# Query order, band factor, store shape and the slot of the mixture in an attention and adapter kernel

## The chip, the cores and the metric

The kernel runs on one core of one Trainium2 chip. The metric is the device time in microseconds (us) of one execution, as the median over runs. A core has five engines with a queue of their own each: TensorE (PE, with its weight loads as PEld), VectorE (DVE), ScalarE (ACT), GpSimd (POOL) and SyncE (SP, which here only issues DMA transfers). An engine works through its queue in order. A wait at the head holds up all that is behind it.

## The reference

Eight batches of eight heads, 576 positions, head dimension 64. Attention with a bias that depends on the distance alone, then per token a mixture of two of eight rank-16 adapters.

```
scores = scale * q @ k^T + bias_table[bucket(|i - j|)]     # bucket is constant from distance 128 on
attn   = softmax(scores);  y = attn @ v
x      = y as (4608 tokens, 512)
logits = x @ w_gate;  keep the two largest of 8;  w = softmax over the two
out    = x + sum over the two of  w_e * (x @ A_e) @ B_e
```

## The kernel before

**Attention.** Heads go in pairs: four pairs to a batch, 32 in all, numbered i, with `hp = i % 4`. The first 512 positions are the main part, the last 64 the tail. The scores of a pair lie transposed, keys on the partitions, in five groups of 1024 columns: groups 0 to 3 are 128 keys each of both heads against 512 queries, group 4 holds the tail keys and the tail queries. PE makes a group (`qk`), ACT takes the exponential (`expo`), DVE multiplies what lies near the diagonal by a band factor exp(bias) (`band`), PE multiplies with V (`pv`), and DVE divides (`recip`, `norm`) into a tile `x` of the batch.

**Order of positions.** A load gives partition p the four positions 4p to 4p+3 (j = 0 to 3), and PE transposes each j by itself (`transposes`). K and Q were both put back into natural order there: column 32j+u of a block of 128 is the position 4u+j of that block. So a batch's output rows lie j by j, and four stores are needed for two blocks (`m_out`).

**The loop.** It runs over slots n = 5i + g, g from 0 to 4, one per group. In what follows (hp, g) names a slot of a batch. Each slot says which instructions are recorded, and each engine's queue is in the order of the recording: no scheduler changes it. Engines have no clock of slots: SP, PE and DVE run ahead until a wait stops them.

**The mixture** of batch b is spread over the slots of the following batches by a table of events (`mixture`): when the last pair of b is done, in slot (0, 4) of batch b+1, one DMA on SP transposes x into `xT` (`m_xdma`; the last batch does it with 16 PE transposes and two DVE copies instead, `m_x`). Then, before the change: `m_logits` in (2, 0), the gates in (2, 2) to (2, 4), `m_z` in (3, 0) and (3, 2), `m_zT` in (3, 4), and in batch b+2 `m_out` in (0, 0), (0, 2), (1, 0), (1, 2). For every second batch the tails of two batches are done together (`m_xtail`, and `m_outt` with its tile `ot`).

**Loads.** SP issues in each batch, for the batch after it: K and Q (1 MB each), V in 16 pieces of 64 KB, 8 of them in slot (0, 0), 4 in (1, 0) and 4 in (2, 0). The same queue holds the xT transposes and all stores. Eight semaphores are handed out in turn to the DMAs of SP and ACT, and a DMA waits until the one eight places ahead of it has landed. POOL casts K, Q and V to bf16 (`cast_kq`, `cast_v`): V of pair i+1 in the last slot of pair i, ahead of the gate's own last step, which is also on POOL.

**The start.** The band factor goes through DRAM: DVE builds a small table (`g_sb`), ACT takes its exponential (`ge`), stores it (`g_d`), SP loads it back shifted by partition (`Mr`), and DVE or POOL copy it in order (`bias_pair`) into `M`. Half of the first batch's V was loaded from ACT's queue.

Of the kernel before, what the change touches and what calls it, by code (L numbers as in the profile page):

```python
# [27 lines left out]
def kernel(  # L28
# [14 lines left out]
    nc = tc.nc  # L43
    B, H, S, D = q.shape
# [8 lines left out]
    S4 = 512  # L53
    MW = 384
# [3 lines left out]
    cp = ctx.enter_context(tc.tile_pool(name="const", bufs=1))  # L58
# [6 lines left out]
    op = ctx.enter_context(tc.tile_pool(name="outs", bufs=3))  # L65
# [3 lines left out]
    ident = cp.tile([128, 128], BF16, tag="ident")  # L69
# [16 lines left out]
    dve = Recorder(nc.vector)  # L86
# [41 lines left out]
    def load_tail(b, w, e):  # L128
        sr = (k, q, v)[w][b, :, S4:, :].rearrange("(c e) p d -> e p c d", e=2)
        s = slice(e * 64, (e + 1) * 64)  # L130
        o = (tls[b % 2][s, w, :, s] if w < 2 else
             vts[b % 2][s, :, e * D1:e * D1 + D])
        nc.gpsimd.dma_start(out=o, in_=sr[e])
# [3 lines left out]
    def cast_kq(i, w, eng=None):  # L137
        b, hp = divmod(i, HP)
        if w == 0:
            kqn[i] = knp.tile([128, 2, 4, 2, D], BF16, name="kqn", tag="kqn")  # L140
        o = kqn[i][:, w].rearrange("p j h d -> p h j d")
        s = kfs[b][w][:, 2 * hp:2 * hp + 2, :].rearrange("p h (j d) -> p h j d", j=4)
        if eng is nc.scalar:
            for h in range(2):
                nc.scalar.copy(o[:, h], s[:, h])
        else:
            return (eng or nc.gpsimd).tensor_copy(o, s)  # L147
# [8 lines left out]
    btT = cp.tile([H, NB], FP32, tag="btT")  # L156
    nc.sync.dma_start(out=btT, in_=bias_table.rearrange("b h -> h b"))
    load_kq(0, 0, 2)
    load_v(0, (0, 1), nc.scalar)
    for t in tls[:1] + vts[:1]:  # L160
        dve.memset(t, 0.0)
    dve.memset(vns[0][:, :, :, D:D1], 1.0)
    for w in range(2):
        for e in range(2):
            load_tail(0, w, e)
    load_kq(0, 2, 4)
    load_v(0, (2, 3))
    load_kq(0, 4, 6)
# [24 lines left out]
    for bv, lo, hi in runs[nsm:]:  # L193
        n = hi - lo
# [6 lines left out]
    g_d = nc.dram_tensor("g_d", (H, 512), BF16, kind="Internal")  # L201
    nc.scalar.dma_start(out=g_d.ap(), in_=ge)
    cast_kq(0, 0, dve)
    cast_kq(0, 1, nc.scalar)
    cast_kq(1, 0, dve)
    cast_kq(1, 1, dve)
    gt = g_d.ap()
# [1 line left out]
    Mr = cp.tile([128, H, MW], BF16, tag="Mr")  # L209
    MHr = cp.tile([128, HP, 192], BF16, tag="MHr")  # L210
    for h0, h1 in ((0, 2), (2, 4), (4, H)):
        for j in range(4):
            nc.sync.dma_start(
                out=Mr[j * 32:(j + 1) * 32, h0:h1, :],
                in_=bass.AP(tensor=gt.tensor, offset=gt.offset + h0 * 512 + j,
                            ap=[[4, 32], [512, h1 - h0], [1, MW]]))
        if h0 == 0:
            for e in range(2):
                nc.sync.dma_start(
                    out=MHr[e * 64:(e + 1) * 64],  # L220
# [4 lines left out]

    M = cp.tile([128, H, 3, 128], BF16, tag="M")
    M4 = cp.tile([128, HP, 256], BF16, tag="M4")
    MHT = cp.tile([128, HP, 2, 64], BF16, tag="MHT")  # L230

    def at(t, off, *dims):
        return bass.AP(tensor=t.tensor, offset=t.offset + off,
                       ap=[t.ap[0]] + [list(d) for d in dims])

    def bias_pair(hp, eng):
        for blk in (1, 2, 0):
            eng.tensor_copy(
                M[:, 2 * hp:2 * hp + 2, blk, :].rearrange("p h (j u) -> p h j u", j=4),
                at(Mr, 2 * hp * MW + MW - 1 - 128 * blk, (MW, 2), (-1, 4), (-4, 32)))  # L240
        eng.tensor_copy(
            M4[:, hp, 0:128].rearrange("p (j u) -> p j u", j=4),
            at(MHr, hp * 192 + 191, (-1, 4), (-4, 32)))
        eng.tensor_copy(
            M4[:, hp, 128:256].rearrange("p (h t) -> p h t", h=2),
            at(Mr, 2 * hp * MW + 127, (MW, 2), (-1, 64)))
        if hp == 0:
            eng.tensor_copy(MHT, at(MHr, 63, (192, HP), (0, 2), (-1, 64)))
# [42 lines left out]
    def transposes(i):  # L291
        n = kqn.pop(i)
        ps = acp.tile([128, 2, S4], BF16, name="kqps", tag="acc")
        for w in range(2):
            for j in range(4):
                o = ps[:, w].rearrange("p (t j u) -> p t j u", t=4, j=4)
                nc.tensor.transpose(o[:, :, j, :], n[:, w, j], ident)  # L297
        t = kqp.tile([128, 2, S4], BF16, name="kqT", tag="kqT")
        dve.tensor_copy(t, ps)
        kqT[i] = t  # L300
# [52 lines left out]
    def band(n):  # L353
        i, g = divmod(n, 5)
        b, hp = divmod(i, HP)
        p = probs[(i, g)]
        if g == 4:
            dve.tensor_tensor(p[:, 384:640], p[:, 384:640], M4[:, hp, :], op=ALU.mult)
            return
        pm = p.rearrange("p (h q) -> p h q", h=2)  # L360
        b0, b1 = max(0, g - 1), min(4, g + 2)
        x0 = b0 - (g - 1)
        Mh = M[:, 2 * hp:2 * hp + 2].rearrange("p h k q -> p h (k q)")
        o = pm[:, :, b0 * 128:b1 * 128]
        dve.tensor_tensor(o, o, Mh[:, :, x0 * 128:(x0 + b1 - b0) * 128], op=ALU.mult)


    pvs = {}
# [160 lines left out]
    def m_out(b, t):  # L529
        zT = st[(b, "zT")]  # L530
        ps = acp.tile([128, Dm], FP32, name="dl", tag="acc")
        nc.tensor.matmul(ps, lhsT=zT[:, t, :], rhs=Bb, start=True, stop=True)  # L532
        if t == 0:
            st[(b, "o")] = op.tile([128, 4, Dm], FP32, name="o", tag="o")
        o = st[(b, "o")]
        dve.tensor_tensor(o[:, t], ps, xs[b][:, t].rearrange("p h d -> p (h d)"),
                          op=ALU.add)
        if t % 2 == 1:
            n0 = b * S + (t - 1) * 128
            orr = out[n0:n0 + 256, :].rearrange("(t u j) d -> j u t d", t=2, j=4)  # L540
            for j in range(4):
                nc.sync.dma_start(out=orr[j], in_=o[j * 32:(j + 1) * 32, t - 1:t + 1])

    def m_outt(b):
        zT = st[(b, "zT")]
# [16 lines left out]
    def mixture(b):  # L562
        tail = b % 2 == 1
        i0 = HP * (b + 1)

        def at_slot(di, g, f, *a):
            events.setdefault(5 * (i0 + di) + g, []).append((f, a))

        if b < B - 1:
            at_slot(0, 4, m_xdma, b)  # L570
        else:
            at_slot(0, 4, m_x, b, 0)
            at_slot(0, 4, m_x, b, 1)
        if tail:
            at_slot(1, 4, m_xtail, b)
        at_slot(2, 0, m_logits, b)
        for n in range(4):
            at_slot(2, (2, 3, 4, 4)[n], m_gate, b, n)
        at_slot(3, 0, m_z, b, 0, 4)
        if tail:  # L580
            at_slot(3, 2, m_z, b, 4, 5)
        at_slot(3, 4, m_zT, b)
        at_slot(4, 0, m_out, b, 0)
        at_slot(4, 2, m_out, b, 1)
        at_slot(5, 0, m_out, b, 2)
        at_slot(5, 2, m_out, b, 3)
        if tail:
            at_slot(6, 4, m_outt, b)


    NPAIR = B * HP
# [5 lines left out]
    for n in range(NG + 5):  # L597
        i, g = divmod(n, 5)
# [97 lines left out]
```

## Time and profile before

| | |
|---|---|
| median of 3 runs | 240.66 us (239.62 to 241.18) |
| span of the profiled execution, first to last instruction | 235.5 us |
| VectorE busy | 185.3 us, 79% of the span |
| TensorE busy | 178.6 us, 76% |
| ScalarE busy | 160.7 us, 68% |
| GpSimd busy | 101.2 us, 43% |
| share of the chain that ended last: DVE, PE, DMA | 37%, 28%, 20% |
| of it the DMA into xT | 12% |

Only the span of the profiled execution is listed, not its own time by the clock of the runs: the median run is 5.2 us longer than the span, and this is taken as what lies around it. In a row, "mean ns of one" is from an instruction's start to its end; on DVE the next one starts before that end, so the step from start to start is shorter.

### The profile page before, as it was taken

The numbers are of one execution on the slowest core, as the hardware profiler recorded it, in microseconds if no ns is written. First come the engines' busy times: TensorE is split into PE (matmuls) and PEld (weight loads), VectorE is DVE, ScalarE is ACT, GpSimd is POOL, SyncE is SP. The second block draws the span as 40 slices with busy tenths as digits, with TensorE's granted clock in tenths as the row PEclk, the third lists the DMA queues.
The fourth block names the chain that finished last, engine by engine and source line by source line (L and its number), as shares of the span: only waits on it lengthen the run. The fifth ranks groups of instructions, "written<-read, shape, count | busy, mean of one in ns | idle before, by whom it ended". The sixth has DMA issues, their size and how long they took to land.

```text
span 235.5 us, 6536 instructions
## 1 busy us (share of the span) xinstructions
PE 178.6 (76%) x2485; PEld 120.5 (51%) x2496; DVE 185.3 (79%) x540; ACT 160.7 (68%) x180; POOL 101.2 (43%) x195
## 2 busy tenths in 40 slices
PE   0177749886999898869992799989892999986560
PEld 0034426554765665546661576566561766665420
DVE  6329648893999999949895389999993799998770
ACT  0368637994899799936993379988990789892000
POOL 8440797562455455534453144554551543220100
PEclk9998997997999999979997589999996799999957
DMA  6977999999978979964998899896998603810616
GB/s 170 197 177 209 346 154 213 260 143 183 330 95 171 190 206 268 207 146 83 268 190 186 182 263 202 184 180 124 332 153 188 133 0 85 187 42 8 180 38 185
DMA packets 91831, 41.54 MB, mean 176 GB/s; under 512 B 69648, under 2 KB 87192, under 8 KB 91800
## 3 DMA queue, kind: packets, MB, share of 16 engines
q1 hardware_dynamic: 71720, 38.75, 70.0%
q0 software_dynamic: 17888, 1.85, 15.4%
q10 hardware_dynamic: 2192, 0.53, 1.4%
q8 instruction: 19, 0.31, 0.6%
q14 instruction: 12, 0.10, 0.1%
HBM read 29.84 MB, written 9.45 MB: 167 GB/s over the span
## 4 chain that ended last, share of the span: by engine, by line
DVE 37%; PE 28%; DMA 20%; issue 4%; ACT 4%; SPq 2%; POOL 2%; POOLq 0%; DVEq 0%
DVE p L82 12%; DMA xT<-x 12%; PE pv L380 10%; DVE x L82 7%; PE sc L334 7%; DVE o L82 4%; ACT p L350 4%; DMA tl<-in_q_dram 2%; DVE rc L82 2%; DMA vf<-in_v_dram 2%; PE tps L306 2%; PE kqps L297 2%; DMA qf<-in_q_dram 2%; DVE kqT L82 2%; PE zp L511 2%
## 5 line engine op out<-in xcount | busy, mean ns | idle before, releaser
L350 ACT ACTIVATE p<-sc 128x1024 bf16<-128x1024 f32 x160 | 153.3, 1034 | 39.8 <-PE sc L334 30.7
L82 DVE TENSOR_TENSOR p<-p,M 128x512 bf16<-128x512 bf16 (+2 forms) x160 | 73.6, 475 | 0.0
L380 PE MATMUL pv<-vn,p 128*128 128x65 bf16 (+1 forms) x1152 | 62.7, 203 | 1.7 <-DVE p L82 1.7
L380 PEld LDWEIGHTS <-p 128*128 128x128 bf16 x1280 | 53.9, 102 | 12.1 <-issue 11.2
L334 PE MATMUL sc<-kqT 64*128 64x512 bf16 x256 | 52.7, 411 | 8.1 <-ACT p L350 5.2
L147 POOL CAST kqn<-qf 128x512 bf16<-128x512 f32 x29 | 17.8, 613 | 35.5 <-DVE rc L82 33.7
L297 PE MATMUL kqps<-ident,kqn 128*128 128x128 bf16 x256 | 21.6, 230 | 14.2 <-DVE kqn L82 7.9
L152 POOL CAST vn<-vf 128x512 bf16<-128x512 f32 x28 | 17.3, 620 | 30.8 <-DVE p L82 15.7
L380 PE MATMUL pv<-vt,p 128*128 128x130 bf16 x128 | 29.0, 227 | 0.0
L82 DVE COPY kqT<-kqps 128x1024 bf16<-128x1024 bf16 x32 | 21.9, 683 | 8.7 <-PE kqps L297 8.6
L297 PEld LDWEIGHTS <-kqn 128*128 128x128 bf16 x256 | 15.5, 102 | 23.0 <-DVE kqn L82 8.2
L334 PEld LDWEIGHTS <-kqT 64*128 64x128 bf16 x256 | 12.9, 94 | 24.2 <-issue 14.7
L82 DVE TENSOR_TENSOR o<-dl,x 128x512 f32<-128x512 f32 x32 | 21.4, 680 | 1.0 <-PE dl L532 0.7
L147 POOL CAST kqn<-kf 128x512 bf16<-128x512 f32 x29 | 18.0, 622 | 7.3 <-DVE p L82 6.3
L465 PE MATMUL lp<-Wb,xT 128*128 128x8 bf16 x144 | 5.1, 167 | 18.2 <-DMA xT<-x 17.0
L82 DVE TENSOR_TENSOR x<-pv,rc 128x384 bf16<-128x384 f32 x32 | 17.8, 557 | 1.1
L82 DVE RECIPROCAL rc<-pv 128x6 f32<-128x6 f32 x64 | 11.7, 182 | 4.3 <-PE pv L380 4.0
L465 PEld LDWEIGHTS <-xT 128*128 128x128 bf16 x144 | 4.4, 99 | 19.6 <-DMA xT<-x 18.1
L475 POOL TENSOR_TENSOR df<-lg,m 128x32 f32<-128x32 f32 (+1 forms) x8 | 2.1, 261 | 27.8 <-DVE m L82 27.8
L343 PEld LDWEIGHTS <-kqT 128*128 128x128 bf16 x128 | 10.2, 101 | 7.4 <-issue 3.0
L82 DVE COPY tlT<-tps 128x1024 bf16<-128x1024 bf16 x8 | 5.5, 690 | 10.3 <-PE tps L306 10.2
L82 DVE TENSOR_TENSOR x<-pv,rm 128x256 bf16<-128x256 f32 x32 | 13.3, 417 | 0.0
(79 smaller groups left out, 209.4 us busy)
## 6 DMA issues: line engine op xcount, KB each, us to landing
out_dram<-o SPq DMA_DIRECT2D x64, 128.0 KB, 2.4
vf<-in_v_dram SPq DMA_DIRECT2D x120, 64.0 KB, 3.9
kf<-in_k_dram SPq DMA_DIRECT2D x7, 1024.0 KB, 6.4
qf<-in_q_dram SPq DMA_DIRECT2D x7, 1024.0 KB, 10.5
kf<-in_k_dram SPq DMA_DIRECT2D x4, 256.0 KB, 3.2
qf<-in_q_dram SPq DMA_DIRECT2D x4, 256.0 KB, 3.7
out_dram<-ot SPq DMA_DIRECT2D x8, 128.0 KB, 2.3
vf<-in_v_dram ACTq DMA_DIRECT2D x8, 64.0 KB, 4.5
```

The costliest lines, as they stand in the source:

```text
L82: self.last = f(*a, **kw)
L147: return (eng or nc.gpsimd).tensor_copy(o, s)
L152: return (eng or nc.gpsimd).tensor_copy(vns[b % 2][:, :, h, :D], vfs[b][:, :, h, :])
L297: nc.tensor.transpose(o[:, :, j, :], n[:, w, j], ident)
L306: nc.tensor.transpose(ps[:, w, c, :], tls[b % 2][:, w, c, :], ident)
L334: nc.tensor.matmul(sc[:, h * 512:(h + 1) * 512], lhsT=t[s, 0, g * 128:(g + 1) * 128], rhs=t[s, 1, :], start=True, stop=True)
L343: nc.tensor.matmul(sc[:, o:o + 128], lhsT=t[:, 0, j * 128:(j + 1) * 128], rhs=tt[:, 1, hp, :], start=True, stop=True, skip_group_check=True)
L350: nc.scalar.activation(p, scs.pop(n), ACT.Exp, scale=scale)
L380: nc.tensor.matmul(acc[:, k, o:o + n], lhsT=lhsT, rhs=rhs, start=start, stop=stop, skip_group_check=True)
L465: nc.tensor.matmul(lp[:, t, :], lhsT=xT[:, 4 * t + c, :], rhs=Wb[:, c, :], start=first, stop=(c == 3), skip_group_check=True)
L475: nc.gpsimd.tensor_tensor(df, lg, m8[:, :, 0:1].to_broadcast((128, nt, E)), op=ALU.subtract)
L511: nc.tensor.matmul(zp[:, t - t0, :], lhsT=xT[:, 4 * t + c, :], rhs=Ab[:, c, :], start=(t == t0 and c == 0), stop=(c == 3), skip_group_chec ...
```

## The change

Seven edits. Q is left in load order: column 128j+p of a pair's queries is position 4p+j, K stays as it was. So tile j of x holds the rows 4p+j, the store of two tiles is one DMA with 4 KB in a row per partition, and a batch leaves in two stores. The queries within 128 of a key group are now a run of 32 to 96 columns in each of the four j, so the band factor `M` has four runs of 96 per head and key group instead of three blocks of 128, and `bias_pair` fills it with one copy instead of three. In group 4 the factor falls into two instructions instead of one. The mixture of batches 0 to 5 runs one pair later from the logits on. Batch 6 transposes on PE like batch 7. The first V loads move from ACT's queue to SP's, and a cast of Q from ACT to DVE.

```diff
-    load_v(0, (0, 1), nc.scalar)
...
+    load_v(0, (0, 1))
     load_kq(0, 2, 4)
...
-    cast_kq(0, 1, nc.scalar)
+    cast_kq(0, 1, dve)
...
-        for blk in (1, 2, 0):
-            eng.tensor_copy(
-                M[:, 2 * hp:2 * hp + 2, blk, :].rearrange("p h (j u) -> p h j u", j=4),
-                at(Mr, 2 * hp * MW + MW - 1 - 128 * blk, (MW, 2), (-1, 4), (-4, 32)))
+        eng.tensor_copy(M[:, 2 * hp:2 * hp + 2],
+                        at(Mr, 2 * hp * MW + MW - 1, (MW, 2), (-1, 4), (-4, 96)))
...
-                o = ps[:, w].rearrange("p (t j u) -> p t j u", t=4, j=4)
-                nc.tensor.transpose(o[:, :, j, :], n[:, w, j], ident)
+                o = (ps[:, 0].rearrange("p (t j u) -> p t j u", t=4, j=4)[:, :, j] if w == 0 else
+                     ps[:, 1, j * 128:(j + 1) * 128])
+                nc.tensor.transpose(o, n[:, w, j], ident)
...
-            dve.tensor_tensor(p[:, 384:640], p[:, 384:640], M4[:, hp, :], op=ALU.mult)
+            o = p[:, 0:512].rearrange("p (j q) -> p j q", j=4)[:, :, 96:128]
+            dve.tensor_tensor(o, o, M4[:, hp, 0:128].rearrange("p (j u) -> p j u", j=4),
+                              op=ALU.mult)
+            dve.tensor_tensor(p[:, 512:640], p[:, 512:640], M4[:, hp, 128:256],
+                              op=ALU.mult)
...
-        o = pm[:, :, b0 * 128:b1 * 128]
-        dve.tensor_tensor(o, o, Mh[:, :, x0 * 128:(x0 + b1 - b0) * 128], op=ALU.mult)
+        pm = p.rearrange("p (h j q) -> p h j q", h=2, j=4)
+        b0, b1 = 32 * max(0, g - 1), 32 * min(4, g + 2)
+        x0 = b0 - 32 * (g - 1)
+        o = pm[:, :, :, b0:b1]
+        dve.tensor_tensor(o, o, M[:, 2 * hp:2 * hp + 2, :, x0:x0 + b1 - b0], op=ALU.mult)
...
-            orr = out[n0:n0 + 256, :].rearrange("(t u j) d -> j u t d", t=2, j=4)
-            for j in range(4):
-                nc.sync.dma_start(out=orr[j], in_=o[j * 32:(j + 1) * 32, t - 1:t + 1])
+            orr = out[b * S:b * S + S4, :].rearrange("(p j) d -> p j d", j=4)
+            nc.sync.dma_start(out=orr[:, t - 1:t + 1], in_=o[:, t - 1:t + 1])
...
-        if b < B - 1:
+        if b < B - 2:
             at_slot(0, 4, m_xdma, b)
...
-        at_slot(2, 0, m_logits, b)
+        d = 3 if b < B - 2 else 2
+        at_slot(d, 0, m_logits, b)
...
-        at_slot(3, 0, m_z, b, 0, 4)
+        at_slot(d + 1, 0, m_z, b, 0, 4)
...
-        at_slot(5, 2, m_out, b, 3)
+        at_slot(d + 3, 2, m_out, b, 3)
         if tail:
-            at_slot(6, 4, m_outt, b)
+            at_slot(d + 4, 4, m_outt, b)
```

What this does to the queues is shown at three places. The first is SP from the tail store of batch 1 (`ot`) on: loads for batch 5 (`kf`, `qf`, `vf`), the transpose of batch 3 (`xT`), the stores of batch 2 (`o`). Before:

```order
L557 DMA out_dram<-ot 64x512 x2
L106 DMA kf<-in_k_dram 128x8x256
L106 DMA qf<-in_q_dram 128x8x256
L114 DMA vf<-in_v_dram 32x8x64 x8
L542 DMA out_dram<-o 32x2x512 x4
L432 DMA_TRANSPOSE xT<-x 128x16x128
L114 DMA vf<-in_v_dram 32x8x64 x4
L542 DMA out_dram<-o 32x2x512 x4
L114 DMA vf<-in_v_dram 32x8x64 x4
```

And in the changed kernel:

```order
L557 DMA out_dram<-ot 64x512 x2
L106 DMA kf<-in_k_dram 128x8x256
L106 DMA qf<-in_q_dram 128x8x256
L114 DMA vf<-in_v_dram 32x8x64 x8
L434 DMA_TRANSPOSE xT<-x 128x16x128
L114 DMA vf<-in_v_dram 32x8x64 x4
L542 DMA out_dram<-o 128x1024
L114 DMA vf<-in_v_dram 32x8x64 x4
L542 DMA out_dram<-o 128x1024
```

Stores of an older batch no longer stand ahead of the transpose, and each is one DMA. The tail store, which before was recorded in slot (2, 4), is now recorded in (3, 4), still ahead of the next batch's loads.

The second is POOL around the gate of batch 1 (`mk`, `gate`); `vn_94` and `vn_97` are the two bf16 V tiles, of batches with even and odd numbers. Before:

```order
L489 TENSOR_TENSOR mk<-mk,ex 128x40
L152 CAST vn_94<-vf 128x4x2x64
L497 TENSOR_TENSOR gate<-mk,sm 128x40
L147 CAST kqn<-kf 128x2x4x64
L147 CAST kqn<-qf 128x2x4x64
L152 CAST vn_97<-vf 128x4x2x64
```

And in the changed kernel:

```order
L491 TENSOR_TENSOR mk<-mk,ex 128x40
L152 CAST vn_97<-vf 128x4x2x64
L499 TENSOR_TENSOR gate<-mk,sm 128x40
L147 CAST kqn<-kf 128x2x4x64
L133 DMA tl_92<-in_k_dram 64x4x64
```

The gate now stands behind the first cast of the next batch's V, where before it stood behind the last cast of the batch at hand.

The third is DVE around the logits of batch 2 (`lg`) and the transposed tail of the next batch (`tlT`). Before:

```order
L82 COPY kqT<-kqps 128x1024
L82 COPY lg<-lp 128x32
L82 MAX m_2000<-lg 128x8 x4
L82 TENSOR_TENSOR mk<-lg,m_2000 128x32
L82 TENSOR_TENSOR p_1961<-p_1961,M 128x2x256
L82 TENSOR_TENSOR p_2012<-p_2012,M 128x2x384
L82 COPY tlT<-tps 128x1024
```

And in the changed kernel, where `tlT` stands a pair ahead of this piece:

```order
L82 TENSOR_TENSOR p_2060<-p_2060,M_181 128x4x32
L82 TENSOR_TENSOR p_2060<-p_2060,M_181 128x128
L82 COPY kqT<-kqps 128x1024
L82 COPY lg<-lp 128x32
L82 MAX m_2106<-lg 128x8 x4
L82 TENSOR_TENSOR mk<-lg,m_2106 128x32
L82 TENSOR_TENSOR p_2070<-p_2070,M 128x8x64
L82 TENSOR_TENSOR p_2118<-p_2118,M 128x8x96
L82 RECIPROCAL rc<-pv 128x6
```

The logits no longer stand in the same pair as the tail's transposes, group 4's band is two rows, and the bands of groups 0 to 3 have eight runs of 64 or 96 in place of two of 256 or 384.

## Rows read from the trace of the kernel before

**Rows 1.** Page, part 1: busy time, share and count of each engine.

```profile
PE 178.6 (76%) x2485; PEld 120.5 (51%) x2496; DVE 185.3 (79%) x540; ACT 160.7 (68%) x180; POOL 101.2 (43%) x195
```

**Rows 2.** Waits: waiting engine and line, releaser, us in total, times, longest.

```profile
PE lp L465 <- DMA xT<-x: 17.0, 6, 5.6
DVE lg L82 <- PE lp L465: 12.3, 5, 4.5
...
DVE tlT L82 <- PE tps L306: 10.2, 6, 3.5
```

**Rows 3.** Timeline of DVE around one stall: start, duration, instruction, [idle before, releaser].

```profile
126.22 0.28 DVE L82 TENSOR_TENSOR p<-p,M 128x256 bf16<-128x256 bf16 x1
126.41 0.69 DVE L82 COPY kqT<-kqps 128x1024 bf16<-128x1024 bf16 x1
131.62 0.20 DVE L82 COPY lg<-lp 128x40 f32<-128x40 f32 x1 [4.52 <-PE lp L465]
...
134.88 0.69 DVE L82 COPY tlT<-tps 128x1024 bf16<-128x1024 bf16 x1 [1.48 <-PE tps L306]
```

**Rows 4.** Windows just after that stall: busy per engine, then granted PE clock, DMA.

```profile
131.50:135.00 3.50, 3.50 (x41) 2.47 (x38) 1.83 (x10) 2.17 (x3) 0.91 (x2) 0.50 0.95 212
```

**Rows 5.** Timeline of DVE, first tail transpose of the run.

```profile
34.76 0.69 DVE L82 COPY tlT<-tps 128x1024 bf16<-128x1024 bf16 x1 [3.48 <-PE tps L306]
```

**Rows 6.** Timeline of SP from the first tail store to the last V loads.

```profile
109.55 1.20 SPq L557 DMA_DIRECT2D out_dram<-ot  x2
...
113.13 10.55 SPq L114 DMA_DIRECT2D vf<-in_v_dram  x8
123.78 2.21 SPq L542 DMA_DIRECT2D out_dram<-o  x4
126.10 2.58 SPq L432 DMA_TRANSPOSE xT<-x  x1
...
132.76 2.07 SPq L114 DMA_DIRECT2D vf<-in_v_dram  x4
```

**Rows 7.** Timeline of PE, the logits behind that transpose.

```profile
130.89 0.69 PE L465 MATMUL lp<-Wb,xT 128*128 128x8 bf16 x20 [5.57 <-DMA xT<-x]
```

**Rows 8.** Timeline of SP from the second tail store on.

```profile
160.93 1.15 SPq L557 DMA_DIRECT2D out_dram<-ot  x2
...
164.84 8.42 SPq L114 DMA_DIRECT2D vf<-in_v_dram  x8
```

**Rows 9.** Tile vf, the V loads: shortest, median and longest time to landing.

```profile
DMA to landing us min/median/max: 1.9/4.0/10.4
```

**Rows 10.** Groups of DVE by form: shapes, count, busy us, mean ns of one.

```profile
L82 DVE TENSOR_TENSOR p<-p,M 128x768 bf16<-128x768 bf16 x64 | 35.7, 559 | 0.0
L82 DVE TENSOR_TENSOR p<-p,M 128x512 bf16<-128x512 bf16 x64 | 27.9, 436 | 0.0
...
L82 DVE TENSOR_TENSOR o<-dl,x 128x512 f32<-128x512 f32 x32 | 21.4, 680 | 1.0 <-PE dl L532 0.7 <-remote 0.3
...
L82 DVE TENSOR_TENSOR zt<-zp,gate 128x512 bf16<-128x512 f32 x8 | 5.5, 684 | 0.7 <-POOL gate L497 0.7
```

**Rows 11.** Timeline of DVE, the last batch's transposed x.

```profile
217.75 1.28 DVE L82 COPY xT<-xps 128x1024 bf16<-128x1024 bf16 x2
```

**Rows 12.** Timeline of ACT at the start.

```profile
0.74 7.87 ACTq L114 DMA_DIRECT2D vf<-in_v_dram  x8
```

**Rows 13.** Timeline of SP at the start.

```profile
3.48 8.64 SPq L114 DMA_DIRECT2D vf<-in_v_dram  x8
...
13.25 1.80 SPq L213 DMA_DIRECT2D Mr<-g_d  x4
```

**Rows 14.** Timeline of SP at the end.

```profile
231.47 1.11 SPq L557 DMA_DIRECT2D out_dram<-ot  x2
```

**Rows 15.** Windows at the end, columns as in rows 4; the last is GB/s.

```profile
229.00:233.00 4.00, 0.00 (x0) 0.00 (x0) 0.64 (x1) 0.00 (x0) 0.00 (x0) 0.93 0.92 257
```

More of the change, by code (lines that the diff above doesn't have):

```diff
@@ L224 @@
             load_kq(0, 6, H)
-    M = cp.tile([128, H, 3, 128], BF16, tag="M")
+    M = cp.tile([128, H, 4, 96], BF16, tag="M")
     M4 = cp.tile([128, HP, 256], BF16, tag="M4")
@@ L357, in band @@
         if g == 4:
-            dve.tensor_tensor(p[:, 384:640], p[:, 384:640], M4[:, hp, :], op=ALU.mult)
-            return
[L360 to L363, printed above, removed]
-        o = pm[:, :, b0 * 128:b1 * 128]
-        dve.tensor_tensor(o, o, Mh[:, :, x0 * 128:(x0 + b1 - b0) * 128], op=ALU.mult)
+            o = p[:, 0:512].rearrange("p (j q) -> p j q", j=4)[:, :, 96:128]
[3 more added lines that the diff above has]
+                              op=ALU.mult)
+            return
+        pm = p.rearrange("p (h j q) -> p h j q", h=2, j=4)
[3 more added lines that the diff above has]
+        dve.tensor_tensor(o, o, M[:, 2 * hp:2 * hp + 2, :, x0:x0 + b1 - b0], op=ALU.mult)
     pvs = {}
@@ L538, in m_out @@
         if t % 2 == 1:
-            n0 = b * S + (t - 1) * 128
-            orr = out[n0:n0 + 256, :].rearrange("(t u j) d -> j u t d", t=2, j=4)
-            for j in range(4):
-                nc.sync.dma_start(out=orr[j], in_=o[j * 32:(j + 1) * 32, t - 1:t + 1])
+            orr = out[b * S:b * S + S4, :].rearrange("(p j) d -> p j d", j=4)
+            nc.sync.dma_start(out=orr[:, t - 1:t + 1], in_=o[:, t - 1:t + 1])
     def m_outt(b):
@@ L575, in mixture @@
             at_slot(1, 4, m_xtail, b)
-        at_slot(2, 0, m_logits, b)
+        d = 3 if b < B - 2 else 2
+        at_slot(d, 0, m_logits, b)
         for n in range(4):
-            at_slot(2, (2, 3, 4, 4)[n], m_gate, b, n)
-        at_slot(3, 0, m_z, b, 0, 4)
+            at_slot(d, (2, 3, 4, 4)[n], m_gate, b, n)
+        at_slot(d + 1, 0, m_z, b, 0, 4)
         if tail:
[L581 to L585, printed above, removed]
-        at_slot(5, 2, m_out, b, 3)
+            at_slot(d + 1, 2, m_z, b, 4, 5)
+        at_slot(d + 1, 4, m_zT, b)
+        at_slot(d + 2, 0, m_out, b, 0)
+        at_slot(d + 2, 2, m_out, b, 1)
+        at_slot(d + 3, 0, m_out, b, 2)
+        at_slot(d + 3, 2, m_out, b, 3)
         if tail:
-            at_slot(6, 4, m_outt, b)
+            at_slot(d + 4, 4, m_outt, b)
     NPAIR = B * HP
```

## The prediction

> **What bounds the kernel now.** I read the shares first, then the waits, then the timeline around the longest wait. The shares name no single bound: VectorE is busy 185.3 us of 235.5, TensorE 178.6, ScalarE 160.7 [rows 1]. The waits say more. In six batches TensorE stood still for the DMA that transposes x, 17.0 us in all and 5.6 at the longest, and VectorE then waited for the logits (12.3 us in five waits) and, a moment later, for the transposed tails (10.2 us in six) [rows 2]. The timeline shows one such stall. VectorE works without a gap up to the copy at 126.41, then is idle 4.52 us until the logits come at 131.62, works a little, and is idle again for 1.48 us [rows 3]. The second gap belongs to the first: after the pause TensorE ran at a granted clock of 0.50, the lower of its levels, 1.2 GHz, and was busy all of the 3.5 us that follow [rows 4]. Outside these stalls the VectorE rows follow each other without idle time, so VectorE is the bound between them, and what counts is its own work plus these gaps.
>
> TensorE is about 1 us ahead of VectorE: of its wait of 5.57 us [rows 7] 4.52 us arrive on VectorE [rows 3].
>
> **The change part by part.** The sum is made against the span of the profiled execution, 235.5 us; the median of the runs, 240.7, is 5.2 above it, and I add that at the end.
>
> *The mixture one pair later: the stalls go, -19.0 us.* Of VectorE's waits for logits and tails, 12.3 + 10.2 us [rows 2], the one of 3.5 us is at the start, where there is no x yet [rows 5]. That leaves 19.0 us. Some tenths of it lie in the last batch and stay; the waits I put back in the next step are meant to cover them.
>
> *What is late next, +5.3 us.* All of it is on SP's queue. A transpose now has one pair more, but the tail store ot also moves one pair later, from (2, 4) to (3, 4), and the loads of the next batch stand behind it, with the next transpose behind them. From ot to the end of the eight V loads SP took 109.55 to 123.68, 14.1 us, since each of these loads waits for the landing of one issued eight places before, and the K and Q loads are among them [rows 6]. The transpose then follows at once, where before four stores took another 2.2 us [rows 6]. From its issue at 126.10 [rows 6] to the logits at 130.89 [rows 7] are 4.8 us. So x is there 14.1 + 4.8 = 18.9 us after ot. When is it wanted? Without the wait the logits would have run at 130.89 - 5.57 = 125.3 [rows 7], 15.8 us after ot, and the distance is 16 slots before and 16 after ((3, 4) to (3, 0)). With the added VectorE work below and the mixture's pieces spread otherwise I take 16.4. The wait is 2.5 us in place of 5.57. On VectorE that is 2.5 - 1.0 = 1.5, and 1.5 for the restart: 3.0. At the second ot the eight V loads end after 12.3 us [rows 8]: 17.1 against 16.4, within the 1 us that TensorE is ahead, so nothing.
>
> The same queue then brings the last V loads. After the transpose come 2.6 us of its issue, four loads, one store and four loads (2.1, 0.5 and 2.1 us [rows 6]; 0.5 is a quarter of four). The last is issued 21.4 us after ot and lands 1.9 to 4.0 us later [rows 9], at 23.3 to 25.4. The cast on POOL that needs it stands in (3, 4), four slots behind the logits, at 18.9 + 4.0 = 22.9 (a slot is 15.8 / 16, about 1.0). And behind that cast now stands the gate, which VectorE's product zt waits for in the next slot. Before, the cast ahead of the gate read V that had landed long ago. So 0.4 to 2.5 us late, of which about one step is cushion; I take 1.15 for each of the two ot batches. Together 3.0 + 2.3 = 5.3. Ends: 1 us if the DMA is a little quicker, 11 us if both waits come close to today's 4.52 and 1.48 [rows 3]. In the other four batches no ot stands ahead of the loads. There the transposes were issued as soon as x was ready, and the added pair is more than the landing takes.
>
> *Group 4's band in two instructions, +2.1 us.* 256 columns more cost 559 - 436 = 123 ns, 0.48 ns a column [rows 10]. A band of 256 takes 0.19 us from its start to the next start [rows 3], so 0.067 is fixed, and the second instruction adds just that: 32 times 0.067 = 2.1 us, all on the bound engine. If the instructions do not overlap, it is up to 0.16, 5.1 us.
>
> *The bands in runs of 64 and 96, 0 us.* The number of columns is the same. No row shows a product of two bf16 tensors in short runs. The nearest is zt, 512 columns in runs of 16, with 684 ns against 680 for o in one run [rows 10]: 4 ns for 32 runs. That is not at the rate of two a step that the band has, so the other end is that the band loses that rate; it is a rival below. A gain is excluded, since no column is saved.
>
> *Batch 6 transposed on TensorE, +2.0 us.* Two copies on VectorE, 1.28 us as in the last batch [rows 11], and VectorE waits for the first eight transposes; ends 1.3, the copies alone, and 2.8, with a wait like the 1.48 behind eight transposes [rows 3]. Nothing comes back, as batch 6's DMA kept nobody waiting.
>
> *The first loads on one queue, -0.3 us.* ACT spent 7.87 us on eight V loads [rows 12]; the band table's way through DRAM starts earlier now. But its loads (Mr) stand at the end of SP's first loads, at 13.25 [rows 13], and SP gets eight issues more. At 2.07 / 4 = 0.52 us each [rows 6] these are 4.1 us, the upper end. SP's own eight took 8.64 us [rows 13], 1.08 each, half of it waiting, since both queues share the eight semaphores. I take it that the added issues fit into that waiting: 0. The -0.3 is the copy of M in one instruction for three, twice on VectorE: four fixed shares of 0.067. The skill has a rule on this: in the Trainium skill, page "Trainium Kernel Development and Optimization", section "Key Constraints", DMAs from several queues run on the same engines, and a second queue saves only the time of issuing. By that rule the move costs its 4.1 us of issue at the start, and the sum would be 234.5 us instead of 230.4, a rival below; the trace of before agrees that the data did not flow faster for two queues but shows the issue time half hidden.
>
> *The stores, -0.4 us.* 64 issues become 16. On SP that saves some 20 us, but SP is waited for only behind ot, where the 2.2 us are already counted. At the end SP gets to the last ot store at 231.47 [rows 14]; one issue in place of four could bring it up to 1.7 us nearer. But from 229 to 233 the DMA is 92% busy at 257 GB/s [rows 15], so the data are the limit, and I give it 0.4; ends -1.7 and 0.
>
> Q's transposes write the same number of columns, and the loads keep their bytes: 0, within work that runs anyway.
>
> Sum: -19.0 + 5.3 + 2.1 + 2.0 - 0.3 - 0.4 = -10.3. Span 225.2, time **230.4 us**. With the ends taken together as independent the forecast's own range is 225 to 237.
>
> **The rivals.** *The loads become the pace (chance 0.13).* The waits for xT stay as they are in both ot batches (2 x 6.0 us for 3.0), and the V behind them is late by its full 2.5 us each time. For it speaks that SP is busy or waiting through most of a batch and that ot, the loads and the transpose hang on each other; against it, that the stores ahead of the transpose are gone. Then +9.0 and +2.7 on 230.4: 242. Milder forms fill 237 to 242.
>
> *Short runs cost the band its rate (0.06), the one that ends slower.* At one column a step each of 64 bands of 768 gains 0.37 us and each of 64 of 512 0.25: 39 us, 270 us. It decides from 10.3 / 128 = 0.08 us per band on: beyond that the change loses. For it: no row excludes it. Against it: zt's 4 ns.
>
> *SP keeps up everywhere (0.07).* Waits of 1 us in all and the end's full 1.7: 224.8 or less.
>
> *The change does not do what it says:* the mixture is later for batches 0 to 5 only in the queues' order; were TensorE to reach the logits no later than now, since it runs ahead where VectorE lets it, the stalls would stay. The third place of the orders speaks against it: a whole pair of VectorE work stands between. 0.04, about 244 us (19.0 less 5.3 on top).
>
> *The start pays for its issues (0.10).* Eight issues of 0.52 us more on SP put Mr 4.1 us later, and the first bands with it: 234.5 us. For it: SP's order is strict, and Mr is last. Against it: half of SP's 8.64 us was waiting [rows 13]. This is what the rule named above would do here.
>
> The forecast itself has 0.60, with the start's rival, which lies in its range, 0.70.
>
> **Range and chances.** About 1%, 2.4 us, is what a measurement here can tell from no change: 238.3 to 243.1. From 224 to 238.5 lies the forecast's range, the milder half of the slow loads and half of the upside, about 0.8. Faster: the forecast, the upside and part of the milder loads, 0.85. Same: the rest of the loads, 0.07. Slower: 0.08 with the lost rate, stalls that stay and what I do not see.
>
> **What would show it.** VectorE's waits for logits and tails: no more than 5 us together outside the start, all of it around the two ot batches. The wait of zt for the gate: 1 to 3 us, new. Bands of 768 at 0.56 us and of 512 at 0.44, as before; 64 products of 128 columns near 0.22 us. TensorE's clock: fewer stretches at the lower level. Mr's first issue near 13 us. Wrong would make it: bands over 0.64 us, logits that wait over 2 us outside the two ot batches, or Mr after 15 us.

## The result

The changed kernel takes **228.35 us** (median of 5 runs, 227.74 to 230.2) against 239.62 us beside it (5 runs, 239.48 to 241.18): ratio 0.958 [0.951, 0.965], faster by 11.3 us. Medians here and below count every run, ratios leave out those more than 1.5% slower than the fastest of their kernel. Forecast were 230.4 us and a gain of 10.3. The sum came out; several of its terms did not. The profiled execution took 230.2 us, the slowest of the five, with a span of 227.5: its span fell by 8.0 us, and 2.7 us lie around it where I assumed 5.2. In the runs that list both numbers 1.7 to 3.0 us lie around the span, 1.8 in most. By that the profiled execution before took some 237.3 us (an estimate), less than any of the five, so the two spans show only 8.0 of the 11.3 us. The working below stands against the spans.

The page's first part, then the waits, answer to [rows 1, 2].

```profile
PE 176.7 (78%) x2501; PEld 120.0 (53%) x2512; DVE 188.7 (83%) x571; ACT 160.0 (70%) x178; POOL 101.5 (45%) x191
```

```profile
PE tps L305 <- DMA tl<-in_q_dram: 11.3, 4, 6.3
...
DVE tlT L82 <- PE tps L305: 10.9, 6, 5.8
DVE rc L82 <- PE pv L382: 5.1, 14, 0.6
DVE kqn L82 <- DMA kf<-in_k_dram: 4.8, 1, 4.8
DVE M L82 <- DMA Mr<-g_d: 2.2, 1, 2.2
...
DVE zt L82 <- POOL gate L499: 0.6, 2, 0.4
...
DVE lg L82 <- PE lp L467: 0.4, 1, 0.4
```

TensorE waits for no transposed x any more (17.0 us before, and no such row now), and VectorE's wait for logits fell from 12.3 us to 0.4. But its wait for the transposed tails is what it was, 10.9 us for 10.2. Its releaser is the same by name, and the cause is another: TensorE now waits for the *load* of q's tails (tl), 11.3 us in four waits. Before, the tails came late because TensorE ran at its lower level after the stall for x [rows 3, 4].

VectorE's timeline at four places: the start, the first transposed tails, the place of the old 4.52 us stall, the end.

```profile
10.42 0.43 DVE L82 CAST kqn<-kf 128x512 bf16<-128x512 f32 x1 [4.79 <-DMA kf<-in_k_dram]
...
11.88 0.68 DVE L82 COPY kqT<-kqps 128x1024 bf16<-128x1024 bf16 x1
...
19.35 0.56 DVE L82 COPY M<-Mr 128x768 bf16<-128x768 bf16 x1 [2.16 <-DMA Mr<-g_d]
...
38.91 0.69 DVE L82 COPY tlT<-tps 128x1024 bf16<-128x1024 bf16 x1 [5.83 <-PE tps L305]
...
126.54 0.88 DVE L82 TENSOR_TENSOR p<-p,M 128x512 bf16<-128x512 bf16 x2
128.54 0.69 DVE L82 COPY tlT<-tps 128x1024 bf16<-128x1024 bf16 x1 [1.12 <-PE tps L305]
...
222.66 0.69 DVE L82 COPY ot<-dlt 128x512 f32<-128x512 f32 x1
```

SP's queue at the same places, for [rows 6, 13, 14].

```profile
2.19 3.97 SPq L114 DMA_DIRECT2D vf<-in_v_dram  x8
6.43 0.38 SPq L106 DMA_DIRECT2D kf<-in_k_dram  x1
...
14.08 1.87 SPq L213 DMA_DIRECT2D Mr<-g_d  x4
...
113.48 1.19 SPq L557 DMA_DIRECT2D out_dram<-ot  x2
...
116.13 8.53 SPq L114 DMA_DIRECT2D vf<-in_v_dram  x8
124.76 3.09 SPq L434 DMA_TRANSPOSE xT<-x  x1
...
223.38 1.12 SPq L557 DMA_DIRECT2D out_dram<-ot  x2
```

VectorE in the kernel before, the partners of the 11.88, 19.35 and 222.66 above:

```profile
13.09 0.69 DVE L82 COPY kqT<-kqps 128x1024 bf16<-128x1024 bf16 x1 [4.54 <-PE kqps L297]
...
18.32 0.69 DVE L82 COPY M<-Mr 128x256 bf16<-128x256 bf16 x3
...
228.95 0.69 DVE L82 COPY ot<-dlt 128x512 f32<-128x512 f32 x1
```

These rows cut the 8.0 us into three places.

| place | before | after | measured | forecast |
|---|---|---|---|---|
| up to the copy of batch 1's tails | 34.76 | 38.91 | +4.2 | -0.3 |
| from there to the end of the last copy ot | 194.88 | 184.44 | -10.4 | -9.6 |
| from that copy's end to the issue of its store | 1.83 | 0.03 | -1.8 | -0.4 |

The store's landing is the rest (4.0 and 4.1 us). So the middle is what I had worked out, the start and the end are not.

**The start.** The long wait for K at 10.42 costs nothing by itself: the copy behind it (kqT) starts at 11.88, where before it started at 13.09, after a wait of 4.54 us for TensorE. The delay shows at Mr: VectorE copies it into M at 19.35 in place of 18.32. GpSimd's last load of batch 1's q tail is then issued 1.1 us later, before and after:

```profile
28.68 0.62 POOL L133 DMA_DIRECT2D tl<-in_q_dram  x1
```

```profile
29.80 0.61 POOL L133 DMA_DIRECT2D tl<-in_q_dram  x1
```

From there to the copy of the tails are 9.1 us (to 38.91) for 6.1 before (to 34.76 [rows 5]). So of the 4.2 us of the first place 1.1 come from the later start, and 3.0 from a slower way of the tails. In the base, the same kernel run again, that way took 7.6 us (29.12 to 36.71); why it differs is not shown.

**Why the tails are late.** GpSimd issues the two loads of q's tails for the next batch, 32 KB each, in pair 1 of a batch, and TensorE transposes them in pair 2. GpSimd's last issue and TensorE at the place of the old stall, after:

```profile
122.36 0.61 POOL L133 DMA_DIRECT2D tl<-in_q_dram  x1
```

```profile
126.14 0.40 PE L305 MATMUL tps<-ident,tl 128*128 128x128 bf16 x4
128.12 0.38 PE L305 MATMUL tps<-ident,tl 128*128 128x128 bf16 x4 [1.59 <-DMA tl<-in_q_dram]
...
131.41 0.65 PE L467 MATMUL lp<-Wb,xT 128*128 128x8 bf16 x20
```

and before:

```profile
123.71 0.62 POOL L133 DMA_DIRECT2D tl<-in_q_dram  x1
```

```profile
133.81 1.03 PE L306 MATMUL tps<-ident,tl 128*128 128x128 bf16 x8
```

Before, 10.1 us passed from the last issue to the transposes, since the stall for x lay between. Now TensorE is there after 126.14 + 0.40 - 122.36 = 4.2 us, and the data come 1.6 us later. The tile's row on its landings, after:

```profile
DMA to landing us min/median/max: 2.3/5.5/9.3
```

A median of 5.5 us does not fit into 4.2. The Trainium skill, page "DMA: Bandwidth & Descriptors", section "Anatomy of one DMA — SWDGE (gpsimd) path", gives such a transfer about 2.0 us plus its bytes; the shortest of this trace, 2.3 us, agrees, the median is over twice that.

VectorE's groups by form for [rows 10, 11]: shapes, count, busy us, mean ns of one.

```profile
L82 DVE TENSOR_TENSOR p<-p,M 128x768 bf16<-128x768 bf16 x64 | 35.6, 557 | 0.0
L82 DVE TENSOR_TENSOR p<-p,M 128x512 bf16<-128x512 bf16 x64 | 28.0, 438 | 0.0
L82 DVE TENSOR_TENSOR p<-p,M 128x128 bf16<-128x128 bf16 x64 | 15.0, 274 | 0.0
L82 DVE COPY xT<-xps 128x1024 bf16<-128x1024 bf16 x4 | 2.6, 682 | 0.0
```

The bands in runs of 64 and 96 cost what they cost before, 557 ns for 559 and 438 for 436.

### The profile page after: what moved, and what is told of

The parts are those of the page before. It is cut to its first block, busy times and chain, and to the rows that moved or that the text cites. A ratio compares the mean times of both kernels' runs of the same rounds, so it can differ in the third digit from the quotient of the medians.

```text
span 227.5 us, 6531 instructions
## 1 busy us (share of the span) xinstructions
PE 176.7 (78%) x2501; PEld 120.0 (53%) x2512; DVE 188.7 (83%) x571; ACT 160.0 (70%) x178; POOL 101.5 (45%) x191
## 4 chain that ended last, share of the span: by engine, by line
DVE 35%; PE 31%; DMA 17%; ACT 8%; issue 4%; SPq 2%; POOL 1%; POOLq 0%; ACTq 0%; DVEq 0%
DMA tl<-in_q_dram 11%; DVE p L82 11%; PE pv L382 9%; ACT p L349 8%; PE sc L333 7%; DVE x L82 5%; DVE o L82 4%; PE kqps L296 3%; DVE kqT L82 3%; DVE rc L82 2%; DMA qf<-in_q_dram 2%; PE sc L338 2%; PE zp L513 2%; PE sc L342 2%; DMA g_d<-ge 2%
## 5 line engine op out<-in xcount | busy, mean ns | idle before, releaser
L82 DVE TENSOR_TENSOR p<-p,M 128x512 bf16<-128x512 bf16 (+2 forms) x192 | 76.3, 423 | 0.0
L333 PE MATMUL sc<-kqT 64*128 64x512 bf16 x256 | 51.6, 403 | 17.3 <-ACT p L349 8.7
L382 PE MATMUL pv<-vn,p 128*128 128x65 bf16 (+1 forms) x1152 | 61.6, 200 | 0.0
L382 PEld LDWEIGHTS <-p 128*128 128x128 bf16 x1280 | 52.5, 100 | 11.7 <-issue 10.4
L333 PEld LDWEIGHTS <-kqT 64*128 64x128 bf16 x256 | 13.5, 94 | 32.4 <-issue 18.1
L305 PE MATMUL tps<-ident,tl 128*128 128x128 bf16 x64 | 6.4, 236 | 11.3 <-DMA tl<-in_q_dram 11.3
L82 DVE COPY tlT<-tps 128x1024 bf16<-128x1024 bf16 x8 | 5.5, 688 | 10.9 <-PE tps L305 10.9
L338 PE MATMUL sc<-kqT,tlT 128*128 128x512 bf16 x32 | 13.1, 409 | 1.4 <-ACT p L349 1.0
L342 PE MATMUL sc<-tlT,kqT 128*128 128x128 bf16 x128 | 13.3, 231 | 0.0
```

The lines of the kernel that those rows point to most:

```text
L82: self.last = f(*a, **kw)
L305: nc.tensor.transpose(ps[:, w, c, :], tls[b % 2][:, w, c, :], ident)
L333: nc.tensor.matmul(sc[:, h * 512:(h + 1) * 512], lhsT=t[s, 0, g * 128:(g + 1) * 128], rhs=t[s, 1, :], start=True, stop=True)
L338: nc.tensor.matmul(sc[:, 0:512], lhsT=tt[:, 0, hp, :], rhs=t[:, 1, :], start=True, stop=True)
L342: nc.tensor.matmul(sc[:, o:o + 128], lhsT=t[:, 0, j * 128:(j + 1) * 128], rhs=tt[:, 1, hp, :], start=True, stop=True, skip_group_check=True)
L382: nc.tensor.matmul(acc[:, k, o:o + n], lhsT=lhsT, rhs=rhs, start=start, stop=stop, skip_group_check=True)
```

## The experiments

The kernel before, run beside each group, took 238.4 to 239.0 us (medians). A number of a run alone is its median, and a ratio is to the kernel before on the same chip. There were three groups, each on a chip of its own: the mixture alone, the tails early and the two kernels of the start; the base, the mixture back, the third piece and the four stores; and the last four kernels. A difference in us between two groups is therefore also one between chips. In the first group the kernel before ran between 234.86 and 241.03 us, so the ratios of that group are the least certain.

**The base again.** The changed kernel, unedited.

> The changed kernel once more, unedited, as the base for the other kernels on the same chip: 227.5 to 229 us. The kernel with only the mixture later took 229.5 on another chip, the one with the old start 227.9; if either differs from this base by less than 1 us, the other edits of the change are worth nothing in sum (my terms gave them +3.4).

228.44 us (6 runs), ratio 0.960 [0.955, 0.965]. In its profiled execution the copy of batch 1's tails stood at 36.71 in place of 38.91: the start varies by some 2 us. The kernel with the mixture alone is 1.0 us slower by the medians, 2.4 by the ratios (0.970 and 0.960 of about 238.4). So the other edits together won little, if that is clear of the noise at all, where my terms gave them +3.4 us of cost.

**The mixture alone**, in the kernel before:

```diff
-        at_slot(2, 0, m_logits, b)
+        d = 3 if b < B - 2 else 2
+        at_slot(d, 0, m_logits, b)
...
```

> The kernel before with one edit: the mixture of batches 0 to 5 one pair later. Everything else (queues of the first loads, bands, four stores per half, batch 6 by DMA) is as before. Theory A (the shift alone brings the gain, the other edits cost): VectorE's wait for logits falls from 12.3 us to under 4 us. My terms give -19.0 + 5.3 = -13.7 us on 239.6, so 226; and since the changed kernel's trace shows nothing late behind SP, the 5.3 may be less: 220 to 226, faster than the changed kernel's 228.35. Theory B (the two stores are needed as well, since SP issues four stores ahead of each transpose and the eight semaphores go round with them): the wait for logits stays at 5 us or more around the two tail stores, 229 to 235 us, slower than the changed kernel.

229.47 us, ratio 0.970 [0.958, 0.982]; wait for logits 0.3 us. Theory A was right on the wait and too low on the time, B the other way round: the wait went without the merged stores, and the tails stood in its place, 9.1 us in five waits. The shift alone is worth 9 us by the medians (238.52 in its group), 7 by the ratio, of the 10 of the base.

**The mixture back at its place**, in the changed kernel (`d = 2` for all batches).

> The changed kernel with the mixture of all batches at its old place (logits two pairs after the batch); all the other edits stay. Theory A (the shift is the whole gain): the stalls for x are back, VectorE's wait for logits is about 12 us, the tails of q are covered again, and the time is 238 to 242, the kernel before (238 to 240) or a little over it. Theory B (the two stores for eight bring x earlier, 2.2 us behind each tail store, so part of the gain is theirs): the wait for logits is 8 us or less, 233 to 236 us.

236.75 us, ratio 0.991 [0.986, 0.996]. VectorE's waits:

```profile
DVE tlT L82 <- PE tps L305: 9.4, 6, 4.8
DVE lg L82 <- PE lp L467: 9.0, 5, 3.4
```

Between the theories: 9.0 us are less than the 12.3 of before. The gain is in the two batches with a tail store, 1.99 and 2.71 us for 4.52 and 3.64. That fits the merged stores, though the kernel before differs in the other edits too. The shift brings 236.75 - 228.44 = 8.3 us. The waits nearly add up to that: 9.0 + 9.4 less the start's two waits for tails (4.75 and 0.82) is 12.8 us here; in the base logits 0.3 and tails 9.4, less 3.88 and 0.68, are 5.1. The difference is 7.7.

**Tails early**, in the changed kernel:

```diff
-        if g in (1, 3) and hp < 3 and nb < B:
-            load_tail(nb, hp, g // 2)
+        if g in (1, 3) and hp == 0 and nb < B:
+            load_tail(nb, g // 2, 0)
+            load_tail(nb, g // 2, 1)
+        if g in (1, 3) and hp == 1 and nb < B:
+            load_tail(nb, 2, g // 2)
```

> The changed kernel with the loads of the next batch's tails earlier on POOL's queue: k and q in pair 0 of the batch (two loads each in slots 1 and 3), v in pair 1, where now k is in pair 0, q in pair 1 and v in pair 2. Theory A (the stalls for x stood just ahead of the tail transposes and covered the landing of q's tails; with them gone those loads are late): TensorE's wait for the tails of q, 11.3 us in four, goes to under 2 us; VectorE saves its 5.8 at batch 1 and 1.05 + 1.12 + 1.69 + 0.35 later, less some for what is late next: 220 to 224 us. Theory B (the DMA engines are full in those places, so that what lands earlier for q makes K, Q or V of the next batch later): 227 to 229 us, with a new wait for kf, qf or vn of a like size.

224.17 us, ratio 0.946 [0.936, 0.956]: 4.3 us under the base, just above theory A's range and well under theory B's. VectorE's waits and, below, TensorE at the first tail store's batch:

```profile
DVE rc L82 <- PE pv L382: 6.1, 14, 1.2
...
DVE lg L82 <- PE lp L467: 1.8, 2, 1.5
DVE tlT L82 <- PE tps L305: 1.4, 2, 0.8
```

```profile
128.17 0.69 PE L467 MATMUL lp<-Wb,xT 128*128 128x8 bf16 x20 [2.81 <-DMA xT<-x]
```

The tails went from 10.9 (9.4 in the base) to 1.4 us. What is late next is x, at this one place: 2.81 us on TensorE, 1.46 on VectorE at the logits and 1.2 behind them (the longest of the first row). That is the wait that I had forecast for the change itself (2.5, 1.5 and 1.5). In the changed kernel the wait for the tails ahead of it hid it: the logits there run at 131.41, without a wait, 6.65 us after the issue of the transpose (124.76).

**The start as before**, in the changed kernel:

```diff
+    load_v(0, (0, 1), nc.scalar)
...
-    load_v(0, (0, 1))
...
-    cast_kq(0, 1, dve)
+    cast_kq(0, 1, nc.scalar)
```

> The changed kernel with the start as it was: the first eight V loads on ScalarE's queue, and the cast of Q of pair 0 on ScalarE. Theory A (the start cost about 4 us: K of pair 1 is now issued at 6.43 us behind eight V loads, VectorE waits 4.8 us for it, and all that follows is later): first tail transposes of batch 1 back from 38.3 to 34 to 35 us, time 224.5 +- 1. Theory B (the tails of q would have been late anyway, since no other stall covers them now, so the start only shows there): the 4.8 us at K go but come back as a longer wait for the tails of q, 227.5 to 228.5 us.

227.93 us, ratio 0.960 [0.949, 0.972], the base's ratio. VectorE's waits:

```profile
DVE tlT L82 <- PE tps L305: 10.8, 6, 5.1
DVE kqT L82 <- PE kqps L296: 7.6, 3, 4.0
```

Theory B on the time, and its tails: the wait for those of batch 1 is 5.1 us (3.9 in the base). The wait at K (3.5 us in the base) is gone, but 4.0 us for TensorE's transposes stand in its place, the longest of the second row, as in the kernel before (4.54). So that wait was never the price of the start. The copy of batch 1's tails stands at 36.73, in the base at 36.71: the tails set the pace there with either start.

**Only the order of the start's loads**: K and Q of pair 1 ahead of the eight V loads, all on SP.

> The changed kernel with two lines of the start exchanged: K and Q of pair 1 are loaded ahead of the first eight V loads, all still on SP's queue. If the start's cost is the order on the queue (K of pair 1 behind V), the 4.8 us wait at K goes and the time is that of the kernel with the old start, 224.5 +- 1. If it is the added issues on one queue, V, then Mr move as far back as K came forward, VectorE's wait for Mr grows from 2.2 us to 3 to 5, and the time stays at 227 to 229.

229.08 us, ratio 0.966 [0.957, 0.975]. The wait at K moved to V, Mr and MHr:

```profile
DVE M L82 <- DMA Mr<-g_d: 2.8, 1, 2.8
DVE kqT L82 <- PE kqps L296: 2.1, 1, 2.1
DVE vn L82 <- DMA vf<-in_v_dram: 1.7, 1, 1.7
DVE M L82 <- DMA MHr<-g_d: 0.9, 1, 0.9
```

These are 5.4 us for Mr, V and MHr, where the base has 6.0 for K, Mr and MHr (3.5 + 1.3 + 1.2): the order only moves the waits. That the number of issues is the cause is not shown by the time, since with late tails even the old start is not clearly faster.

**A third piece of group 4's band**, in the changed kernel:

```diff
-            dve.tensor_tensor(p[:, 512:640], p[:, 512:640], M4[:, hp, 128:256],
-                              op=ALU.mult)
+            for s in range(2):
+                o = p[:, 512 + 64 * s:576 + 64 * s]
+                dve.tensor_tensor(o, o, M4[:, hp, 128 + 64 * s:192 + 64 * s], op=ALU.mult)
```

> The changed kernel with group 4's second band product cut once more, two instructions of 64 columns for one of 128: 32 instructions more on VectorE, the same columns. It doubles the cost of the split. Theory A (VectorE is the bound almost everywhere): 32 times its fixed share of 0.067 = 2.1 us more, by the listed busy time of the first split (15.0 us for 64 products of 128, against 12.4 for 32 of 256) up to 2.6: +2 to +3 us. Theory B (TensorE and ScalarE are within 10% of VectorE, and VectorE's small pieces come out of its waits for them): VectorE's busy time rises by 2 to 3 us, but its waits for pv fall by as much, and the time by +0 to +0.7.

229.47 us, ratio 0.962 [0.956, 0.968], 1.0 over the base, with overlapping intervals. The three products list 10.2 + 9.0 us of busy time, the two of the base 16.3: 2.9 more. The waits for pv did not fall (4.8 us, 3.4 in the base), so B's reason is not seen; A's size is not reached either. A split costs between 0 and 2 us, not settled more closely.

**Four stores per half**, in the changed kernel:

```diff
-            nc.sync.dma_start(out=orr[:, t - 1:t + 1], in_=o[:, t - 1:t + 1])
+            for j in range(4):
+                s = slice(j * 32, (j + 1) * 32)
+                nc.sync.dma_start(out=orr[s, t - 1:t + 1], in_=o[s, t - 1:t + 1])
```

> The changed kernel with each half batch's store cut in four by partitions: 64 issues for 16, the same bytes, rows and run lengths. Theory A (only what stands behind a tail store and the very end see SP's issues): xT's issue comes 1.5 to 2.2 us later at two places; since x had about 1 us to spare there, the wait for logits grows to 1 to 3 us, and the end by up to 0.5: +1 to +3 us. Theory B (SP has room all along): no wait for logits, +0 to +0.5 us. If it is more than +4, the merged stores were a main part of the gain.

230.76 us, ratio 0.967 [0.961, 0.974], 2.3 over the base. The intervals overlap a little (the base has [0.955, 0.965]). No row for logits is longer than in the base; the size is A's, its place is not. The last copy and its store:

```profile
221.32 0.69 DVE L82 COPY ot<-dlt 128x512 f32<-128x512 f32 x1
```

```profile
223.87 1.12 SPq L559 DMA_DIRECT2D out_dram<-ot  x2
```

The copy ends at 222.01 and SP comes to its store 1.86 us later, still issuing the four quarters of the half before. In the base it is 0.03 us (copy to 220.75, store at 220.78).

**Batch 6 by DMA**, in the changed kernel (`if b < B - 1` for the DMA, the old place of its mixture).

> The changed kernel with batch 6's x transposed by DMA again, its mixture still two pairs after the batch. My terms gave batch 6 on TensorE +2.0 us, of which two copies on VectorE are 1.36. Theory A (the copies lie on the bound engine and the DMA of batch 6 keeps nobody waiting, since no loads are left ahead of it but those of batch 7): 226 to 227 us. Theory B (with the old place of its logits, batch 6 by DMA has the stall that the other batches had, 2 to 3 us for x and 1 to 1.5 for the restart): the wait for logits at about 195 us is back with 1.5 to 3 us and the time is 228.5 to 230.5.

226.86 us, ratio 0.949 [0.944, 0.955]. SP's issue and the logits of batch 6:

```profile
189.91 1.76 SPq L434 DMA_TRANSPOSE xT<-x  x1
```

```profile
195.27 0.55 PE L467 MATMUL lp<-Wb,xT 128*128 128x8 bf16 x16
```

No stall, as theory A has it, and 1.6 us less in the median than the base on another chip, whose interval [0.955, 0.965] touches this one. The last kernel below does not repeat the gain.

**Tails early and the old start together.**

> The changed kernel with the tails loaded early and the start's queues as before, together. The early tails alone gave 224.2. If the start's waits at K of pair 1 (3.0 us) and Mr (2.6) are on the path once the tails do not wait, the time falls by 2 to 3 more, to 221 to 222. If the start is bound by the DMA engines' bytes, whatever the queue, it stays at 223.5 to 224.5.

222.06 us, ratio 0.930 [0.927, 0.934]. With early tails alone, on another chip, it was 224.17 us and 0.946 [0.936, 0.956]. The copy of batch 1's tails stands at 32.42, with early tails alone at 33.82. So the old start is worth 1.4 us at that place and 2.1 in the medians once the tails no longer wait. VectorE's copy of Mr, with early tails alone and here:

```profile
19.84 0.56 DVE L82 COPY M<-Mr 128x768 bf16<-128x768 bf16 x1 [2.61 <-DMA Mr<-g_d]
```

```profile
18.59 0.55 DVE L82 COPY M<-Mr 128x768 bf16<-128x768 bf16 x1
```

Here 1.25 of the 1.4 us are already gained. Both kernels with the old start move the V loads and the cast of Q back together; the two were not run apart.

**Weights one pair later as well**:

```diff
-        if 10 <= n < 15:
-            load_weights(n - 10)
+        if 15 <= n < 20:
+            load_weights(n - 15)
```

> As the one before, with the five weight loads one pair later (slots 15 to 19 in place of 10 to 14). They come in pieces of 32 bytes and fill the DMA engines at 30 to 38 us, beside the V loads of batch 1, which take 17 us there. If that is what holds the start, K of batch 2 and with it the next loads come 2 to 3 us sooner and the time falls by 0.5 to 2 us; if nobody waits for those V loads, 0; if the weights now meet the loads of batch 2 at 42 us and make x of batch 0 late, +1 to +2.

221.29 us (220.35 to 221.74), ratio 0.927 [0.924, 0.930], 0.8 less than the one before on the same chip (221.41 to 222.82). But not for the reason given: the sixteen V loads of batch 1, which I thought the weights held up, took longer. Without the later weights, then with them:

```profile
22.72 14.21 SPq L114 DMA_DIRECT2D vf<-in_v_dram  x16
```

```profile
22.15 16.86 SPq L114 DMA_DIRECT2D vf<-in_v_dram  x16
```

K of batch 2 is issued 2.1 us later, not earlier (39.11 for 37.03). In the two profiled executions TensorE's wait for x falls from 3.7 to 0.5 us and the copy of batch 1's tails is 1.1 us earlier (31.33 for 32.42). The two kernels' runs and intervals overlap, and what gave the 0.8 us stays open.

**And batch 6 by DMA on top.**

> Early tails, the old start, weights one pair later, and batch 6 by DMA, as the candidate for the best version: the sum of what the three beside it show, 220 to 222 if each gives its share; 223 to 225 if batch 6 by DMA stalls at its logits.

222.75 us (219.99 to 225.16), ratio 0.926 [0.920, 0.932]: no better than without. The kernel with early tails, the old start and later weights has the lowest median of this study, 7.1 us under the changed kernel and 17.7 under the kernel before (239.01 beside it).

## Why the prediction came out

*The stalls go, -19.0 us:* right in its mechanism. The waits for x (17.0 us) and logits (12.3 us, 0.4 left) are gone, and the shift alone does it. The size holds 1.1 us that could not go: a second wait for tails at the start, 0.81 us in both kernels, and the last batch's logits, 0.3 us. What could go was 17.9 us.

*What is late next, +5.3 us:* the size right, the place wrong. I looked for the next late thing on SP's queue alone and put 3.0 us on x and 2.3 on the gate. On the gate VectorE waits 0.6 us in all, and the 0.7 of before shows that this wait was not new [rows 10]. Left outside the start and the last batch are 10.9 - 5.83 - 0.81 = 4.2 us, all for the tails, whose q half comes on GpSimd's queue. So -17.9 + 4.2 = -13.7 us, the very sum of my two terms (-19.0 + 5.3): luck, since the wait that came is not the one I priced. The step that failed is the reading of VectorE's second gap as a mere consequence of the first: while the stall stood ahead of it, it also gave the tails' loads 10.1 us to land, and their landing (a median of 4.5 us before) was never set against the time that would be left without it, 4.2. The wait for x is real, but only the kernel with early tails shows it.

*Split band, +2.1 us:* busy time rose by 15.0 - 12.4 = 2.6 us (12.4 is 32 times the 387 ns of a band of 256 before), and one product of 128 columns lists 0.274 us where I looked for 0.22; one more split cost 1.0 us in the median, 0 not excluded.

*Bands in short runs, 0:* right, 557 and 438 ns; the rival that ended slower needed 0.08 us a band.

*Batch 6 on TensorE, +2.0 us:* the two copies are there (2 of the 4 of 682 ns, 1.36 us). Undone, it gave 1.6 us once, between two chips, and nothing once.

With the split and the copies taken in full, the middle nearly closes: -13.7 + 2.6 + 1.4 = -9.7 of the -10.4 measured.

*The start, -0.3 us:* wrong, and in the sign. The path was the one I followed, Mr's; the step that failed is that the added issues fit into SP's waiting. Mr's first issue came 0.8 us later (14.08 for 13.25; 2.0 between the two kernels with early tails, 15.37 for 13.40) and its copy on VectorE 1.0. The rest of the 4.2 us at the start of the profiled execution is not the price of the queue but that of the tails: their copy stood at 36.71 in the base, and at 36.13 in the kernel with the mixture alone, whose start is the old one. Freed of them, the price is 1.4 us at that copy and 2.1 us in the medians of the two kernels with early tails. The rival of the paid issues (+4.1 us) was nearer in kind.

The rule I set beside it, from the Trainium skill, page "Trainium Kernel Development and Optimization", section "Key Constraints", is that a second issuing engine saves issue time and nothing else. The runs agree as far as they go: with early tails the old start won 1.4 to 2.1 us, less than the 4.1 us of issue. The other order on one queue was run only with late tails, where the old start won nothing clear either.

*The stores, -0.4 us:* too small, for a wrong reason. I saw the DMA engines 92% busy at the end [rows 15] and took the bytes for the limit. The last tail store waited for SP: 1.83 us before, 0.03 after, which is the end of the range (-1.7) that I had turned down. Four stores again bring back 1.86.

So the total was near because errors cancelled. In the profiled execution (230.2 us) the start was 4.5 us dearer than forecast, the end 1.4 and the middle 0.8 better, and 2.5 us less lay around the span than assumed. Between whole kernels it is the same: the shift alone won 7 to 9 us, not 13.7 (in its profile VectorE's waits for logits and tails fell by 12.6 us outside the start and the last batch, the span by 10.4: not every wait that goes comes back as time), and the other edits together 1 to 2.4 us, hardly clear of the noise, where I had them cost 3.4.

## What to carry to other kernels

A stall is also cover: whatever is loaded ahead of it on any queue has had the stall's time to land, so before removing it compare, for every later consumer, the time from issue to use without the stall with the landing times in the trace. When a long wait is removed and another of the same size appears under an old name, look one releaser further back: the same row of VectorE hid a clock that was low before and a late load after. At the end of a kernel look at the issuing queue before the bandwidth: here the last store waited 1.83 us behind other issues, though the engines that carry it were 92% busy.

## What the runs showed of the hardware

TensorE's clock does not fall at every wait. Windows of the changed kernel behind two waits for the tails, of 1.59 us (until 128.12) and 2.07 us (until 174.76); the column behind POOL's is the granted clock:

```profile
128.20:131.20 3.00, 2.75 (x42) 1.90 (x42) 2.59 (x8) 1.65 (x2) 1.16 (x2) 1.00 0.99 204
174.80:177.80 3.00, 3.00 (x33) 2.32 (x33) 2.41 (x5) 0.87 (x1) 1.16 (x2) 0.56 0.90 159
```

Behind the first it stayed at 1.00 (2.4 GHz), behind the second it was 0.56, most of the window at the lower level (1.2 GHz), as behind the stall of 5.57 us before [rows 4]. These are three waits, and no more is read from them. Over whole executions the mean granted clock is higher without the stalls: 0.884 to 0.910 in 11 runs of the kernel before, 0.953 to 0.974 in 6 runs of the kernel with the lowest median, on the same chip.
